# A squeeze-and-excitation block on one core: rows moved 32 at a time instead of 8, cut into small pieces only around the gate

## The chip, the cores and the metric

One core of a Trainium2 chip. The time is the device time of one execution in microseconds; a kernel is judged by the median of its executions. Most executions of one kernel agree closely; a run that is more than 1.5% above the fastest of its kernel is called slow and left out of comparisons.

## The reference

`x` has 256 x 256 pixels of 384 channels in bf16, 50.3 MB. The mean over all pixels goes through two tiny layers and a sigmoid, which gives one factor per channel; every pixel is then multiplied by these factors.

```python
def reference(x, w_down, w_up):
    s = x.mean(axis=(1, 2))
    s = _sigmoid(_silu(s @ w_down) @ w_up)       # 384 -> 24 -> 384
    return x * s[:, None, None, :]
```

No output can be written before all of `x` has been read once. `x` doesn't fit on the core, so a part has to be read a second time.

## The kernel before

A partition holds 512 pixels (called rows here: one row is 384 channels on each of 128 partitions, 98,304 bytes). The kernel works in chunks of 8 rows. 33 chunks (264 rows) have their own slot in SBUF and stay there; the other 31 chunks (248 rows) pass through the same slots first and are read again at the end. The sums over pixels are made by matmuls against a column of ones, one per row.

```python
    JS = 8 if J >= 64 else max(1, J // 8)
    chunks = [(j0, min(JS, J - j0)) for j0 in range(0, J, JS)]
    ...                                       # n_slots comes out as 33, NS as 31
    for (ch, sl) in p1_order:                 # 31 streamed chunks, then 33 that stay
        j0, jsz = chunks[ch]
        st = slots[sl]
        nc.sync.dma_start(out=st[:, :jsz, :], in_=x3[:, j0:j0 + jsz, :])
        for jj in range(jsz):
            ...                               # one matmul per row into sums_ps
    ...
    # the gate: mean (VectorE), transpose (TensorE), copy (VectorE), first layer (TensorE),
    # sigmoid (ScalarE), z1a and z1bc (VectorE), second layer (TensorE), sigmoid (ScalarE)
    def scale_and_store(sl, ch):
        j0, jsz = chunks[ch]
        st = slots[sl]
        gate_b = gate[:, None, :].to_broadcast([P, jsz, C])
        nc.vector.tensor_tensor(
            out=st[:, :jsz, :], in0=st[:, :jsz, :], in1=gate_b, op=ALU.mult
        )
        nc.scalar.dma_start(out=out3[:, j0:j0 + jsz, :], in_=st[:, :jsz, :])

    for i in range(n_slots):
        scale_and_store(i, cache_ids[i])
    for k in range(NS):
        sl = k % n_slots
        j0, jsz = chunks[stream_ids[k]]
        nc.sync.dma_start(out=slots[sl][:, :jsz, :], in_=x3[:, j0:j0 + jsz, :])
        scale_and_store(sl, stream_ids[k])
```

## Time and profile before

The median is 313.33 us (14 executions, 313.16 to 313.70).

| stretch of the profiled execution | us | what limits it |
|---|---|---|
| start to the last load's landing | 125.5 | reading 512 rows, 50.3 MB |
| last landing to the first store's issue | 6.2 | the chain of small steps that makes the gate |
| first store's issue to the end | 180.0 | writing 512 rows and reading 248 again, 74.7 MB |

First come lines of the page of the kernel before. The two long rows are the 40 slices of the span: the busy share of the DMA engines in tenths, and GB/s. Then the shares of the chain that ended last, by engine. Then two groups of instructions (line, engine, operation, output and inputs, count; then busy time in us and mean ns). Last are the DMA issues by line, with count, KB of one and us to landing.

```profile
span 311.8 us, 1476 instructions
...
DMA  7999999999999998099999999999999999999997
GB/s 286 414 417 415 417 419 418 416 418 416 418 415 415 420 418 349 1 365 419 423 419 425 427 422 424 428 423 423 428 426 421 427 426 423 427 426 423 425 427 313
...
DMA 76%; DVE 5%; PE 1%; issue 0%; ACTq 0%; ACT 0%; SPq 0%
...
L175 DVE TENSOR_TENSOR slot<-slot,gate 128x3072 bf16<-128x3072 bf16 x64 | 107.8, 1753 | 20.0 <-DMA slot<-in_x_dram 19.0
L91 PE MATMUL sums_ps<-slot,ones_bf 128*1 128x384 bf16 x512 | 95.4, 331 | 31.7 <-DMA slot<-in_x_dram 31.6
...
slot<-in_x_dram SPq DMA_DIRECT2D x95, 768.0 KB, 15.0
out_dram<-slot ACTq DMA_DIRECT2D x64, 768.0 KB, 14.7
```

The DMA is saturated in every slice but the first, the two in the middle and the last, and most of the chain is transfers. VectorE and TensorE work about 100 us each, hidden behind the transfers. So there are two things to win: a better rate in the 36 good slices, or a shorter hole in the middle.

The stretches view of the kernel before: stretch in us, its length, busy time and (count) of PE, PEld, DVE, ACT and POOL, the granted clock of TensorE (as a share of its full clock), the DMA share (how busy the 16 DMA engines are on average; 1.00 is always) and GB/s. The first stretch is pure reading, the second the first 8 us of stores, the third pure writing.

```profile
20.00:100.00 80.00, 60.65 (x334) 27.70 (x333) 0.00 (x0) 0.00 (x0) 0.00 (x0) 1.00 1.02 417
132.00:140.00 8.00, 0.00 (x0) 0.00 (x0) 8.00 (x6) 0.00 (x0) 0.00 (x0) 0.50 0.94 343
265.00:295.00 30.00, 0.00 (x0) 0.00 (x0) 0.00 (x0) 0.00 (x0) 0.00 (x0) 0.50 1.02 425
```

417 GB/s is the rate of reading, 425 of writing. The hole, as the chain that ended last shows it (start us, us, what):

```profile
110.56 14.99 DMA slot<-in_x_dram
...
125.59 1.47 PE sums_ps L91 x8
...
127.08 0.56 DVE mean_bf L108
...
129.45 0.50 ACT gate L167
...
129.97 11.78 DVE slot L175 x7
```

The last load lands at 125.54 us. Eight matmuls for its rows follow (1.47 us), then the mean and the small steps up to 129.95, then multiplies. Only after the first multiply of 8 rows can the first store go; the timeline of the kernel before has it (start, us, engine, line, operation):

```profile
131.76 21.18 ACTq L178 DMA_DIRECT2D out_dram<-slot  x10
```

131.76 - 125.54 = 6.22 us without any transfer in progress, apart from the latencies at both sides.

### The profile page before, as it was taken

How to read it: one execution, taken by the hardware profiler on the slowest of the kernel's cores; microseconds unless marked ns; L12 is line 12 of the kernel's file. 1: busy time of each engine (PE TensorE's matmuls, PEld its weight loads, DVE VectorE, ACT ScalarE, POOL GpSimd, SP SyncE). 2: the span in 40 equal slices, each digit the busy share in tenths (PEclk: the TensorE clock that was granted, in tenths of full speed). 3: DMA queues.
4: the chain of work that ended last, by engine and by line, in shares of the span. 5: the costliest groups of instructions: out<-in, count | busy, mean ns of one | idle time of the engine just before them, and what ended most of it. 6: DMA issues, size and time to landing. Idle time of an engine off the chain costs nothing.

```text
span 311.8 us, 1476 instructions
## 1 busy us (share of the span) xinstructions
PE 96.1 (31%) x519; PEld 43.7 (14%) x519; DVE 109.0 (35%) x69; ACT 1.9 (1%) x3; POOL 0.2 (0%) x4
## 2 busy tenths in 40 slices
PE   3976777777777777300000000000000000000000
PEld 1432333333333333100000000000000000000000
DVE  0000000000000000499999999999555540000000
ACT  1000000000000000000000000000000000000000
POOL 0000000000000000000000000000000000000000
PEclk9999999999999999855555555555555555555555
DMA  7999999999999998099999999999999999999997
GB/s 286 414 417 415 417 419 418 416 418 416 418 415 415 420 418 349 1 365 419 423 419 425 427 422 424 428 423 423 428 426 421 427 426 423 427 426 423 425 427 313
DMA packets 23371, 125.18 MB, mean 402 GB/s; under 512 B 2988, under 2 KB 3012, under 8 KB 23364
## 3 DMA queue, kind: packets, MB, share of 16 engines
q1 hardware_dynamic: 13680, 74.72, 58.2%
q10 hardware_dynamic: 9684, 50.37, 39.1%
q8 instruction: 4, 0.07, 0.1%
q14 instruction: 3, 0.02, 0.0%
HBM read 74.75 MB, written 50.33 MB: 401 GB/s over the span
## 4 chain that ended last, share of the span: by engine, by line
DMA 76%; DVE 5%; PE 1%; issue 0%; ACTq 0%; ACT 0%; SPq 0%
DMA slot<-in_x_dram 40%; DMA out_dram<-slot 33%; DVE slot L175 4%; DMA wd_sb<-in_w_down_dram 3%; PE sums_ps L91 0%; ACTq L102 0%; DVE mean_bf L108 0%; ACT gate L167 0%; PE zz_ps L160 0%; DVE z1bc L149 0%; PE meanT_ps L118 0%; PE z_ps L136 0%; DVE meanT_sb L127 0%; ACT s L144 0%; DVE z1a L146 0%
## 5 line engine op out<-in xcount | busy, mean ns | idle before, releaser
L175 DVE TENSOR_TENSOR slot<-slot,gate 128x3072 bf16<-128x3072 bf16 x64 | 107.8, 1753 | 20.0 <-DMA slot<-in_x_dram 19.0
L91 PE MATMUL sums_ps<-slot,ones_bf 128*1 128x384 bf16 x512 | 95.4, 331 | 31.7 <-DMA slot<-in_x_dram 31.6
L91 PEld LDWEIGHTS <-ones_bf 128*1 128x1 bf16 x512 | 43.3, 85 | 83.4 <-issue 48.0
L108 DVE TENSOR_SCALAR mean_bf<-sums_ps 1x384 bf16<-1x384 f32 x1 | 0.5, 546 | 126.1 <-PE sums_ps L91 126.1
L144 ACT ACT_TABLE_LOAD x1 | 1.3, 1283 | 3.1 <-issue 3.1
L144 ACT ACTIVATE s<-z_ps 24x1 f32<-24x1 f32 x1 | 0.2, 160 | 124.0 <-PE z_ps L136 124.0
L160 PE MATMUL zz_ps<-wu_sb,z1bc 24*128 24x384 bf16 x1 | 0.3, 332 | 0.7 <-DVE z1bc L149 0.7
L167 ACT ACTIVATE gate<-zz_ps 128x384 bf16<-128x384 f32 x1 | 0.5, 491 | 0.9 <-PE zz_ps L160 0.9
L71 DVE MEMSET ones_bf<- 128x128 bf16 x1 | 0.2, 165 | 0.8 <-PEq L201 0.8
L118 PE MATMUL meanT_ps<-ones_bf,mean_bf 1*128 1x1 bf16 x3 | 0.2, 163 | 0.6 <-DVE mean_bf L108 0.6
L146 DVE TENSOR_TENSOR z1a<-z_ps,s 24x1 f32<-24x1 f32 x1 | 0.1, 145 | 0.5 <-ACT s L144 0.5
L136 PE MATMUL z_ps<-meanT_sb,wd_sb 128*24 128x1 bf16 x3 | 0.2, 163 | 0.3 <-DVE meanT_sb L127 0.3
L118 PEld LDWEIGHTS <-mean_bf 1*128 1x128 bf16 x3 | 0.1, 91 | 1.0 <-DVE mean_bf L108 1.0
L127 DVE CAST meanT_sb<-meanT_ps 128x3 bf16<-128x3 f32 x1 | 0.2, 162 | 0.3 <-PE meanT_ps L118 0.3
L149 DVE TENSOR_SCALAR z1bc<-ones_bf,z1a 24x128 bf16<-24x128 bf16 x1 | 0.2, 242 | 0.0
L136 PEld LDWEIGHTS <-wd_sb 128*24 128x24 bf16 x3 | 0.2, 89 | 0.3 <-issue 0.2
L160 PEld LDWEIGHTS <-z1bc 24*128 24x128 bf16 x1 | 0.1, 91 | 0.8 <-DVE z1bc L149 0.8
L201 POOL MEMSET const-uint8-127<- 128x1 uint8 x1 | 0.1, 102 | 0.0
L201 POOL MEMSET const-bfloat16-1.0<- 128x1 bf16 x1 | 0.1, 101 | 0.0
L201 POOL MEMSET const-float32-0.0<- 128x1 f32 x1 | 0.1, 98 | 0.2 <-issue 0.2
L201 POOL MEMSET const-float32-1.0<- 128x1 f32 x1 | 0.1, 98 | 0.0
## 6 DMA issues: line engine op xcount, KB each, us to landing
slot<-in_x_dram SPq DMA_DIRECT2D x95, 768.0 KB, 15.0
out_dram<-slot ACTq DMA_DIRECT2D x64, 768.0 KB, 14.7
wd_sb<-in_w_down_dram ACTq DMA_DIRECT2D x3, 6.0 KB, 6.2
wu_sb<-in_w_up_dram ACTq DMA_DIRECT2D x1, 18.0 KB
```

Source lines behind the costliest of these rows:

```text
L71: nc.vector.memset(ones_bf[:], 1.0)
L91: nc.tensor.matmul(sums_ps[ci][:1, :csz], ones_bf[:, 0:1], st[:, jj, c0:c0 + csz], start=first, stop=last,)
L108: nc.vector.tensor_scalar(out=mean_bf[:1, c0:c0 + csz], in0=sums_ps[ci][:1, :csz], scalar1=1.0 / float(N), scalar2=None, op0=ALU.mult,)
L118: nc.tensor.matmul(meanT_ps[:csz, kt:kt + 1], mean_bf[0:1, c0:c0 + csz], ones_bf[0:1, 0:1], start=True, stop=True,)
L127: nc.vector.tensor_copy(out=meanT_sb[:, :], in_=meanT_ps[:, :])
L136: nc.tensor.matmul(z1_ps[:R, 0:1], wd_sb[:csz, kt, :], meanT_sb[:csz, kt:kt + 1], start=(kt == 0), stop=(kt == KT - 1),)
L144: nc.scalar.activation(out=s1[:R, :], in_=z1_ps[:R, :], func=ACT.Sigmoid)
L149: nc.vector.tensor_scalar(out=z1bc[:R, :], in0=ones_bf[:R, :], scalar1=z1a[:R, 0:1], scalar2=None, op0=ALU.mult,)
L160: nc.tensor.matmul(zz_ps[:, :csz], z1bc[:R, :], wu_sb[:R, c0:c0 + csz], start=True, stop=True,)
L167: nc.scalar.activation(out=gate[:, c0:c0 + csz], in_=zz_ps[:, :csz], func=ACT.Sigmoid)
L175: nc.vector.tensor_tensor(out=st[:, :jsz, :], in0=st[:, :jsz, :], in1=gate_b, op=ALU.mult)
L201: nc = _bacc.Bacc("TRN2", target_bir_lowering=False, num_devices=1)
```

## The change

The intent: move 32 rows with one DMA, so that each of the 128 runs is 24,576 bytes long and not 6,144, and cut the DMAs and multiplies into small pieces only where somebody waits for the first one (the end of the first pass, the first stores, the first re-reads). The gate's small steps go to ScalarE, one of them is fused, a warm-up activation loads the sigmoid's table at the start, and the two weights move to another queue. The cached and the twice-read rows stay 264 and 248.

```diff
-    JS = 8 if J >= 64 else max(1, J // 8)
+    JS = 32
+    n_slots = 264 // JS
+    spare = 8                     # rows of one more, smaller slot
 ...
+    warm = consts.tile([1, 1], BF16)
+    nc.scalar.activation(out=warm[:], in_=ones_bf[0:1, 0:1], func=ACT.Sigmoid)
 ...
+    for n, (ch, sl) in enumerate(p1_order):
+        remaining = len(p1_order) - n
+        pieces = {1: [4, 2, 2], 2: [8, 8, 8, 4, 4], 3: [16, 16]}.get(remaining)
+        read_and_reduce(ch, sl, pieces)          # one DMA per piece
 ...
-        nc.scalar.dma_start(out=wd_sb[:csz, kt, :], in_=w_down[c0:c0 + csz, :])
+        nc.gpsimd.dma_start(out=wd_sb[:csz, kt, :], in_=w_down[c0:c0 + csz, :])
 ...
-        nc.vector.tensor_scalar(out=mean_bf..., in0=sums_ps..., scalar1=1.0 / float(N), op0=ALU.mult)
+        nc.scalar.activation(out=mean_bf..., in_=sums_ps..., func=ACT.Copy, scale=1.0 / float(N))
 ...
-    nc.vector.tensor_tensor(out=z1a..., in0=z1_ps..., in1=s1..., op=ALU.mult)
-    nc.vector.tensor_scalar(out=z1bc..., in0=ones_bf..., scalar1=z1a..., op0=ALU.mult)
+    nc.scalar.activation(out=z1bc..., in_=z1_ps[:R, 0:1].to_broadcast([R, P]),
+                         func=ACT.Copy, scale=s1[:R, 0:1])
 ...
+    for i in range(n_cache):                      # one multiply and one store per piece
+        scale_and_store(i, cache_ids[i], piece_rows={0: [2, 2, 4, 4, 4, 8, 8],
+                                                     1: [8, 8, 16], 2: [16, 16]}.get(i))
     for k in range(NS):
+        for rsz in {0: [4, 4, 8, 16], 1: [16, 16]}.get(k, [jsz]):   # re-reads
```

More of the change, by code (lines that the diff above doesn't have):

```diff
@@ L36 @@
     cn_chunks = [(c0, min(512, C - c0)) for c0 in range(0, C, 512)]
-    JS = 8 if J >= 64 else max(1, J // 8)
-    chunks = [(j0, min(JS, J - j0)) for j0 in range(0, J, JS)]
-    NCH = len(chunks)
-    bytes_per_slot = JS * C * 2
-    small_bytes = (
-        C * 2
-        + 256
-        + max(32, ((KT * R * 2 + 31) // 32) * 32)
-        + C * 2
-        + C * 2
-        + 8 * 32
-    )
-    avail = nc.sbuf_top - nc.sbuf_base
-    n_slots = max(2, min(NCH, (avail - small_bytes - 2048) // bytes_per_slot))
-    NS = NCH - n_slots
+    JS = 32
+    HALF = JS // 2
+    n_slots = 264 // JS
+    spare = 8
+    cached_rows = n_slots * JS + spare
+    NS = -(-(J - cached_rows) // JS)
+    sizes = [JS] * NS
+    sizes[-1] = J - cached_rows - JS * (NS - 1)
+    sizes += [JS] * n_slots + ([spare] if spare else [])
+    chunks, r = [], 0
+    for sz in sizes:
+        chunks.append((r, sz))
+        r += sz
+    assert r == J
+    NCH = len(chunks)
+    n_cache = NCH - NS
     stream_ids = list(range(NS))
@@ L68 @@
     ]
+    if spare:
+        slots.append(slots_pool.tile([P, spare, C], BF16, name="slot_spare"))
     ones_bf = consts.tile([P, P], BF16)
     nc.vector.memset(ones_bf[:], 1.0)
+    warm = consts.tile([1, 1], BF16)
+    nc.scalar.activation(out=warm[:], in_=ones_bf[0:1, 0:1], func=ACT.Sigmoid)
     sums_ps = [
@@ L78, with read_and_reduce @@
     p1_order = [(stream_ids[k], k % n_slots) for k in range(NS)] + [
-        (cache_ids[i], i) for i in range(n_slots)
+        (cache_ids[i], i) for i in range(n_cache)
     ]
     total_mm = J
-    mm_idx = 0
-    for (ch, sl) in p1_order:
+    mm_state = {"idx": 0}
+    def read_and_reduce(ch, sl, pieces):
         j0, jsz = chunks[ch]
         st = slots[sl]
-        nc.sync.dma_start(out=st[:, :jsz, :], in_=x3[:, j0:j0 + jsz, :])
-        for jj in range(jsz):
-            first = mm_idx == 0
-            last = mm_idx == total_mm - 1
-            for ci, (c0, csz) in enumerate(cn_chunks):
-                nc.tensor.matmul(
-                    sums_ps[ci][:1, :csz],
-                    ones_bf[:, 0:1],
-                    st[:, jj, c0:c0 + csz],
-                    start=first,
-                    stop=last,
-                )
-            mm_idx += 1
+        cuts = []
+        r = 0
+        for pr in pieces or [jsz]:
+            cuts.append((r, pr))
+            r += pr
+        assert r == jsz
+        for (r0, rsz) in cuts:
+            nc.sync.dma_start(
+                out=st[:, r0:r0 + rsz, :], in_=x3[:, j0 + r0:j0 + r0 + rsz, :]
+            )
+            for jj in range(r0, r0 + rsz):
+                first = mm_state["idx"] == 0
+                last = mm_state["idx"] == total_mm - 1
+                for ci, (c0, csz) in enumerate(cn_chunks):
+                    nc.tensor.matmul(
+                        sums_ps[ci][:1, :csz],
+                        ones_bf[:, 0:1],
+                        st[:, jj, c0:c0 + csz],
+                        start=first,
+                        stop=last,
+                    )
+                mm_state["idx"] += 1
@@ L100 @@
+    for n, (ch, sl) in enumerate(p1_order):
+        remaining = len(p1_order) - n
+        pieces = {1: [4, 2, 2], 2: [8, 8, 8, 4, 4], 3: [16, 16]}.get(remaining)
+        read_and_reduce(ch, sl, pieces)
     wd_sb = consts.tile([P, KT, R], BF16)
     for kt, (c0, csz) in enumerate(ck_chunks):
-        nc.scalar.dma_start(out=wd_sb[:csz, kt, :], in_=w_down[c0:c0 + csz, :])
+        nc.gpsimd.dma_start(out=wd_sb[:csz, kt, :], in_=w_down[c0:c0 + csz, :])
     wu_sb = consts.tile([R, C], BF16)
-    nc.scalar.dma_start(out=wu_sb[:R, :], in_=w_up[:, :])
+    nc.gpsimd.dma_start(out=wu_sb[:R, :], in_=w_up[:, :])
@@ L106 @@
     mean_bf = work.tile([1, C], BF16)
     for ci, (c0, csz) in enumerate(cn_chunks):
-        nc.vector.tensor_scalar(
+        nc.scalar.activation(
             out=mean_bf[:1, c0:c0 + csz],
-            in0=sums_ps[ci][:1, :csz],
-            scalar1=1.0 / float(N),
-            scalar2=None,
-            op0=ALU.mult,
+            in_=sums_ps[ci][:1, :csz],
+            func=ACT.Copy,
+            scale=1.0 / float(N),
         )
@@ L126 @@
     if all(csz == P for (c0, csz) in ck_chunks):
-        nc.vector.tensor_copy(out=meanT_sb[:, :], in_=meanT_ps[:, :])
+        nc.scalar.activation(out=meanT_sb[:, :], in_=meanT_ps[:, :], func=ACT.Copy)
     else:
         for kt, (c0, csz) in enumerate(ck_chunks):
-            nc.vector.tensor_copy(
-                out=meanT_sb[:csz, kt:kt + 1], in_=meanT_ps[:csz, kt:kt + 1]
+            nc.scalar.activation(
+                out=meanT_sb[:csz, kt:kt + 1], in_=meanT_ps[:csz, kt:kt + 1],
+                func=ACT.Copy,
             )
@@ L144 @@
     nc.scalar.activation(out=s1[:R, :], in_=z1_ps[:R, :], func=ACT.Sigmoid)
-    z1a = work.tile([R, 1], FP32)
-    nc.vector.tensor_tensor(out=z1a[:R, :], in0=z1_ps[:R, :], in1=s1[:R, :], op=ALU.mult)
     z1bc = work.tile([R, P], BF16)
-    nc.vector.tensor_scalar(
+    nc.scalar.activation(
         out=z1bc[:R, :],
-        in0=ones_bf[:R, :],
-        scalar1=z1a[:R, 0:1],
-        scalar2=None,
-        op0=ALU.mult,
+        in_=z1_ps[:R, 0:1].to_broadcast([R, P]),
+        func=ACT.Copy,
+        scale=s1[:R, 0:1],
     )
@@ L169, with scale_and_store @@
         )
-    def scale_and_store(sl, ch):
+    def scale_and_store(sl, ch, piece_rows=None):
         j0, jsz = chunks[ch]
         st = slots[sl]
-        gate_b = gate[:, None, :].to_broadcast([P, jsz, C])
-        nc.vector.tensor_tensor(
-            out=st[:, :jsz, :], in0=st[:, :jsz, :], in1=gate_b, op=ALU.mult
-        )
-        nc.scalar.dma_start(out=out3[:, j0:j0 + jsz, :], in_=st[:, :jsz, :])
-    for i in range(n_slots):
-        scale_and_store(i, cache_ids[i])
+        if piece_rows is None:
+            cuts = [(0, jsz)]
+        else:
+            cuts = []
+            r = 0
+            for pr in piece_rows:
+                if r >= jsz:
+                    break
+                pr = min(pr, jsz - r)
+                cuts.append((r, pr))
+                r += pr
+            if r < jsz:
+                cuts.append((r, jsz - r))
+        for (r0, rsz) in cuts:
+            gate_b = gate[:, None, :].to_broadcast([P, rsz, C])
+            nc.vector.tensor_tensor(
+                out=st[:, r0:r0 + rsz, :],
+                in0=st[:, r0:r0 + rsz, :],
+                in1=gate_b,
+                op=ALU.mult,
+            )
+            nc.scalar.dma_start(
+                out=out3[:, j0 + r0:j0 + r0 + rsz, :], in_=st[:, r0:r0 + rsz, :]
+            )
+    for i in range(n_cache):
+        scale_and_store(i, cache_ids[i], piece_rows={0: [2, 2, 4, 4, 4, 8, 8], 1: [8, 8, 16], 2: [16, 16]}.get(i))
     for k in range(NS):
@@ L184 @@
         j0, jsz = chunks[stream_ids[k]]
-        nc.sync.dma_start(out=slots[sl][:, :jsz, :], in_=x3[:, j0:j0 + jsz, :])
+        r0 = 0
+        for rsz in {0: [4, 4, 8, 16], 1: [16, 16]}.get(k, [jsz]):
+            nc.sync.dma_start(
+                out=slots[sl][:, r0:r0 + rsz, :], in_=x3[:, j0 + r0:j0 + r0 + rsz, :]
+            )
+            r0 += rsz
+        assert r0 == jsz
         scale_and_store(sl, stream_ids[k])
```

## The prediction

> **What bounds it now.** The page shows DMA at 0.9 or more in all but the first and the middle two of its 40 slices, and the chain that ended last is 76% DMA. 125.05 MB have to move (760 rows read, 512 written, 96 KB each). The stretches view gives 417 GB/s in the load pass, 425 afterwards. The one real hole is the gate: in the chain the last load lands at 125.54 us, then eight matmuls (1.47), small steps up to the gate's end at 129.95, one 8-row multiply (1.75), first store issued at 131.76: 6.2 us. Multiplies (107.8 us) and matmuls (95.4) are hidden.
>
> **What stays.** Bytes are the same: 264 rows cached (8 x 32 + 8), 248 read twice. The sigmoid table load is already at 3.1 us, off the path: the warm-up gains nothing. Weights on another queue gain nothing; they are needed at 128 us.
>
> **Gain 1, the rate.** The trace's packet records: every data packet is 6144 B, one per partition and DMA, 234 ns; a 4-byte packet takes 9 ns, a 48-byte one 11, a 768-byte one 36.5: about 8 ns beside its bytes. In steady state one engine's period is 236 ns (loads), 231 ns (stores). The Trainium skill, "DMA: Bandwidth & Descriptors", gives a ceiling of 435 GB/s (section "Where 436 GB/s comes from"), which is 226 ns for 6144 B, and about 3 cycles of overhead per packet (section "Why small descriptors are slow"); the trace agrees with a residue of 5 to 10 ns, semaphores included. With 32 rows a packet is 24576 B if it stays whole, and the residue is paid a quarter as often. Estimate: loads 417 to 430 GB/s (120.7 to 117 us: -3.7), the rest 425 to 432.5 (74.7 MB: -3.0). If rows are split, or the loads' residue is the HBM's, only part comes. Expected: -5.5.
>
> **Gain 2, the hole.** Two matmuls after the last landing, plus a small backlog (104 rows at 162 ns against 72 landing at 229): about 0.6 instead of 1.47. The fused z1bc and the ScalarE copies save 0.2. The Trainium skill, "ScalarE: Activation LUTs", section "Table sets", says that copy is in every set, so I expect no second table load (1.28 us each). First multiply, 2 rows: 0.55 (1753 ns for 3072 elements, about 0.15 fixed) against 1.75. First store 3.9 us after the last landing instead of 6.2. But 2- and 4-row multiplies deliver 3.6 to 4.2 rows/us, less than DMA takes (4.4), so it starves until re-reads come: about 0.6 given back. Net -1.7.
>
> **Not on the path.** When re-reads start doesn't matter much: stores have over 55 us of backlog, and the kernel ends in a pure store stretch.
>
> **Predicted: 305.5 us**, 8 times in 10 between 301 and 311. Chances: faster by over 2% 0.66, within 2% 0.33, slower 0.01.
>
> **What would show it.** Packets of 24576 B; 428 to 432 GB/s in the load pass, 431 to 434 at the end (if still 417 and 425, gain 1 is wrong); last landing to first store 3.6 to 4.3 us; exactly one table load; the first 10 us of stores somewhat below full rate.
>
> **What would make it wrong.** Rows split into packets of the old length. HBM limiting loads to 417. Matmuls in bursts of 32 with 2 us gaps losing the clock (320 ns each, as at the start), so that a backlog stands at the last landing. Re-reads held back by large stores, so that DMA starves on the DVE for longer. A table load between Copy and Sigmoid.

## The result, and the profile after

The changed kernel has a median of 307.00 us (10 executions, 306.21 to 309.64) against 313.33 (14). The ratio is 0.9813, 95% interval 0.9792 to 0.9835. A ratio here is the mean time of one kernel's fast runs over that of the other's of the same rounds, so it is not quite the ratio of the medians. The interval lies on both sides of 2%, so "faster by over 2%" is neither confirmed nor excluded; that it is faster is clear. Two later sets of five executions gave medians of 307.12 and 306.83.

| stretch of the profiled execution | before | after | difference | predicted |
|---|---|---|---|---|
| start to the last load's landing | 125.5 | 122.3 | -3.2 | -3.7 if packets stay whole |
| last landing to first store | 6.2 | 4.0 | -2.3 | -2.3 |
| first store to the end | 180.0 | 178.1 | -1.9 | -3.0 for the rate, +0.6 for starving |
| span | 311.8 | 304.4 | -7.4 | |

The profiled execution took 306.44 us, one of the fast ones; that of the kernel before took 313.53. The time is longer than the span by 1.8 us before and by 2.1 us after, so of the 7.4 us in the span 7.1 are left in the time. Lines of its page, in the order of those before, with the table load added:

```profile
span 304.4 us, 1259 instructions
...
DMA  8999999999999998299999999999999999999997
GB/s 311 417 430 448 410 436 443 413 429 446 413 432 443 407 417 334 99 371 426 422 426 431 459 388 443 417 452 423 423 452 426 420 449 417 433 443 417 455 420 310
...
L204 DVE TENSOR_TENSOR slot<-slot,gate 128x12288 bf16<-128x12288 bf16 (+5 forms) x25 | 103.1, 4186 | 150.6 <-ACT gate L182 124.7
L105 PE MATMUL sums_ps<-slot,ones_bf 128*1 128x384 bf16 x504 | 90.3, 341 | 31.0 <-DMA slot<-in_x_dram 30.8
...
L75 ACT ACT_TABLE_LOAD x1 | 1.3, 1283 | 0.7 <-PEq L241 0.7
...
slot<-in_x_dram SPq DMA_DIRECT2D x18, 3072.0 KB, 35.2
out_dram<-slot ACTq DMA_DIRECT2D x12, 3072.0 KB, 47.2
```

There are fewer and larger DMAs, and still one table load. The packet records of the trace have runs of 24,576 B, 912 ns each when nothing disturbs them, where there were four of 234 ns (936). The stretches view of the changed kernel, in which 127 to 135 is its first 8 us of stores:

```profile
20.00:100.00 80.00, 60.59 (x343) 29.49 (x341) 0.00 (x0) 0.00 (x0) 0.00 (x0) 0.95 1.01 431
127.00:135.00 8.00, 0.00 (x0) 0.00 (x0) 8.00 (x7) 0.00 (x0) 0.00 (x0) 0.50 0.97 340
265.00:295.00 30.00, 0.00 (x0) 0.00 (x0) 0.00 (x0) 0.00 (x0) 0.00 (x0) 0.50 1.00 433
```

Reading went from 417 to 431 GB/s, writing from 425 to 433. The 431 is a little high, because the edges of a stretch cut long DMAs: undo and coarse below read 428 there. A straight line through the bytes of the packet records gives 417.1 before and 429.5 after for reading (the same in undo and coarse to 0.3), and 425.0 and 432.7 for writing. The granted clock of TensorE in the first stretch is no longer 1.00 but 0.95; an experiment below deals with that. The first 8 us of stores run at 340 GB/s, as before (343). Two stretches of the changed kernel and one of the kernel before show more:

```profile
128.00:129.00 1.00, 0.00 (x0) 0.00 (x0) 1.00 (x2) 0.00 (x0) 0.00 (x0) 0.50 0.81 310
130.00:132.00 2.00, 0.00 (x0) 0.00 (x0) 2.00 (x2) 0.00 (x0) 0.00 (x0) 0.50 1.00 255
...
136.00:140.00 4.00, 0.00 (x0) 0.00 (x0) 4.00 (x4) 0.00 (x0) 0.00 (x0) 0.50 1.03 339
```

At first the DMA engines of the changed kernel are in part idle (share 0.81) while VectorE never rests. From 130 us, when its first re-reads begin (130.75), they are busy all the time and yet move only 255 GB/s; the kernel before has the same dip where its re-reads begin (137.48). Nor is VectorE the slower one: its multiplies of 4 rows start 0.87 us apart (4.6 rows/us), those of 8 rows in the kernel before 1.67 us (4.8), and 432.7 GB/s are 4.4 rows/us. So that the DMA starves on VectorE is not shown, and at most a part of the low rate; why the start of the re-reads costs so much is not shown either. The chain of the changed kernel around the gate:

```profile
105.46 15.93 DMA slot_spare<-in_x_dram
...
121.43 1.47 PE sums_ps L105 x8
...
122.93 0.49 ACT mean_bf L127
...
124.39 0.37 ACT z1bc L165
...
125.17 0.50 ACT gate L182
...
125.70 0.04 DVE slot L204
```

The eight matmuls of the last slot start when its first piece lands (121.39); its last piece lands at 122.33, by the landing records, and the matmuls end 0.57 us later. The 24-partition product is one step of 0.37 us now, and the first multiply is one of 2 rows: it starts at 125.70 and takes 0.56 us, of which only the first 0.04 lie on this chain. The first store is issued at 126.29, 3.96 us after the last landing:

```profile
126.29 19.89 ACTq L210 DMA_DIRECT2D out_dram<-slot  x12
```

### The profile page after: what moved, and what is told of

It reads as the page before. It is cut to its first block, busy times and chain, and to the rows that moved or that the text cites. A ratio compares the mean times of both kernels' runs of the same rounds, so it can differ in the third digit from the quotient of the medians.

```text
span 304.4 us, 1259 instructions
## 1 busy us (share of the span) xinstructions
PE 92.6 (30%) x519; PEld 45.0 (15%) x519; DVE 104.9 (34%) x27; ACT 3.1 (1%) x7; POOL 2.5 (1%) x8
## 4 chain that ended last, share of the span: by engine, by line
DMA 62%; DVE 12%; another core or an unknown queue 5%; PE 3%; issue 1%; SPq 1%; ACT 1%; DVEq 0%
DMA slot<-in_x_dram 47%; DVE slot L204 12%; DMA out_dram<-slot 10%; DMA slot_spare<-in_x_dram 5%; PE sums_ps L105 3%; SPq L98 1%; ACT gate L182 0%; ACT mean_bf L127 0%; ACT z1bc L165 0%; PE zz_ps L175 0%; PE meanT_ps L136 0%; PE z_ps L155 0%; DVEq L204 0%; ACT meanT_sb L145 0%
## 5 line engine op out<-in xcount | busy, mean ns | idle before, releaser
L204 DVE TENSOR_TENSOR slot<-slot,gate 128x12288 bf16<-128x12288 bf16 (+5 forms) x25 | 103.1, 4186 | 150.6 <-ACT gate L182 124.7
L105 PE MATMUL sums_ps<-slot,ones_bf 128*1 128x384 bf16 x504 | 90.3, 341 | 31.0 <-DMA slot<-in_x_dram 30.8
L105 PEld LDWEIGHTS <-ones_bf 128*1 128x1 bf16 x512 | 44.6, 87 | 77.9 <-issue 40.8
L121 POOL DMA_DIRECT2D wd_sb<-in_w_down_dram x3 | 1.8, 602 | 0.8 <-POOLq L241 0.8
L204 DVE TENSOR_TENSOR slot_spare<-slot_spare,gate 128x3072 bf16<-128x3072 bf16 x1 | 1.8, 1753 | 0.0
L105 PE MATMUL sums_ps<-slot_spare,ones_bf 128*1 128x384 bf16 x8 | 1.5, 325 | 0.1
L75 ACT ACT_TABLE_LOAD x1 | 1.3, 1283 | 0.7 <-PEq L241 0.7
```

The costliest lines, as they stand in the source:

```text
L75: nc.scalar.activation(out=warm[:], in_=ones_bf[0:1, 0:1], func=ACT.Sigmoid)
L105: nc.tensor.matmul(sums_ps[ci][:1, :csz], ones_bf[:, 0:1], st[:, jj, c0:c0 + csz], start=first, stop=last,)
L121: nc.gpsimd.dma_start(out=wd_sb[:csz, kt, :], in_=w_down[c0:c0 + csz, :])
L204: nc.vector.tensor_tensor(out=st[:, r0:r0 + rsz, :], in0=st[:, r0:r0 + rsz, :], in1=gate_b, op=ALU.mult,)
```

## The experiments

The kernels of one call share the runs of the kernel before: medians of 313.53, 313.46 and 313.42 us. Two of those runs, of 339.65 and 371.07 us, were slow and are left out. The changed kernel itself was repeated for comparison.

**The theory**: most of the gain comes from longer packets, because each packet costs some nanoseconds beside its bytes; the pieces and the shorter chain around the gate add about 1.5 us. **Rivals**: larger DMAs (more bytes in flight, fewer completions) give the rate, not longer packets; or the gain lies around the gate. A second question came with the result: why do the times of the changed kernel spread over 3 us, when those of the kernel before spread over 0.5?

### again and again2: the changed kernel repeated

No edit.

> The changed kernel unchanged, as the measure for the runs beside it. Median near 307.0 us. If the spread of its times (306.2 to 309.6 before) comes from the tensor engine's clock dropping at a different chunk in each execution, the spread comes again, and a second profile shows the drops at other chunks than the first (34, 69 and 98 us).

> The changed kernel once more, as the measure for the runs beside it: median 307.0 us, times from 306.2 to 309.6. In the profile the 16 landings of the last store should lie 0.5 us apart when the execution is a fast one (306.4) and 2 us or more when it is above 307.8, if single DMA engines that fall behind make the spread.

Measured: again 307.12 us (306.86 to 308.75, ratio 0.9809), again2 306.83 us (306.39 to 308.39, ratio 0.9797). The spread came again. The clock drops of again's profile lie at 33 and 84 us, so at other chunks than in the first profile, but both profiles have the same load pass (last landing 122.28 and 122.33 us) and the same hole (3.92 and 3.96). All of the difference lies after the first store: 179.6 us in again, 178.1 in the first. So the drops seen there cost nothing, and something else made again's profiled execution 1.4 us longer.

The landing records show where. Every DMA is split over 16 engines, and each reports its own landing. For the last store of three profiled executions of this one kernel:

```
execution          last landing   last minus first of the 16 landings
306.44 us          303.19 us      0.5 us
306.97 us          303.7 us       1.6 us
307.87 us          304.63 us      2.4 us
```

In the execution of 307.87 us, 15 engines had finished by 303.42 and one came 1.2 us later. The first landing as late as that is at 147.10 us, 3.5 us after the first of its DMA, the 15th only 0.8 after it. The records don't name the engine, so that it is the same one up to the end is an inference. Nor is a delay there always kept: in the execution of 306.44 us the landings of one store lie 2.1 us apart at 140 us, and 0.5 at the end.

In the load pass engines are late too, and there the traces show with what it comes. The 16 landings of one load lie within 0.6 us of each other at first. After each packet of 16,384 B of the queue that the page calls "instruction" (1.0 to 1.1 us long; in the first profile at 30.2, 61.4, 89.7 and 116.5 us) one more of the 16 is about 1.4 us late: one after the first packet, four after the fourth. All 13 profiles of fast executions have this, with that of the kernel before. In warm and best2 below, whose added matmuls bring six such packets, the first at 11 us, the late landings come earlier as well and are five at the end. So the load pass ends on a few engines, as these stretches of the changed kernel show (DMA share 0.36 and 0.21):

```profile
120.00:121.00 1.00, 1.00 (x9) 0.51 (x7) 0.00 (x0) 0.00 (x0) 0.00 (x0) 1.00 0.36 135
121.00:122.00 1.00, 0.88 (x6) 0.40 (x5) 0.00 (x0) 0.00 (x0) 0.00 (x0) 1.00 0.21 78
```

Both kernels pay this, so it is no part of the gain, and no run tried to avoid it. In the three executions of the table no such packet lies between 117 us and the last landing, so the late engine of the stores has another cause.

### p8: short packets, all else kept

```diff
+    PK = 8
 ...                       # the same at loads, stores and re-reads:
-            nc.sync.dma_start(out=st[:, r0:r0 + rsz, :], in_=x3[:, j0 + r0:j0 + r0 + rsz, :])
+            for q in range(r0, r0 + rsz, PK):
+                qe = min(q + PK, r0 + rsz)
+                nc.sync.dma_start(out=st[:, q:qe, :], in_=x3[:, j0 + q:j0 + qe, :])
```

> Every long load, store and re-read cut into DMAs of 8 rows; slots, matmuls, multiplies and the gate untouched. Packet theory (about 5 to 10 ns per packet beside its bytes): the rates fall back to 417 GB/s in the load pass and 425 afterwards, about 6 us, so 312 to 313.5 us. If the gain of the change lay in the hole around the gate instead, this stays at 307 to 308.

Measured: 312.08 us (311.64 to 312.29), ratio 0.9951. The stretches of pure reading and pure writing:

```profile
20.00:100.00 80.00, 60.81 (x334) 27.77 (x334) 0.00 (x0) 0.00 (x0) 0.00 (x0) 1.00 1.02 417
265.00:295.00 30.00, 0.00 (x0) 0.00 (x0) 0.00 (x0) 0.00 (x0) 0.00 (x0) 0.50 1.02 425
```

The rates are exactly those of the kernel before, while the hole stays at 3.97 us. So the pieces and the new chain alone are worth 313.53 - 312.08 = 1.45 us, and long DMAs the other 5 of the 6.4 us.

### pad8: large DMAs with short packets

The DMAs stay at 3 MB; 32 bytes between blocks of 8 rows in SBUF break every run into four.

```diff
-        slots_pool.tile([P, JS, C], BF16, name=f"slot{i}") for i in range(n_slots)
+        slots_pool.tile([P, JS // 8, 8 * C + 16], BF16, name=f"slot{i}") for i in range(n_slots)
 ...                       # and every access to a slot by blocks, for example
-                out=st[:, r0:r0 + rsz, :], in_=x3[:, j0 + r0:j0 + r0 + rsz, :]
+                out=rows(st, r0, rsz), in_=far(x3, j0 + r0, rsz)
```

> DMAs stay as large as in the changed kernel (3 MB), but 32 bytes between blocks of 8 rows in SBUF break each row of 24576 B into four packets of 6144 B. Theory that packet length sets the rate: as slow as with 8-row DMAs less the few semaphore packets, 417 to 419 and 425 to 427 GB/s, 311 to 313 us. Rival, that the size of a DMA (more bytes in flight, fewer completions) sets it: the rates of the changed kernel, 429 to 433 GB/s, 307 us.

Measured: 311.14 us (310.81 to 311.73), ratio 0.9927; the packet records have 6,144 B again. The stretches:

```profile
20.00:100.00 80.00, 61.41 (x339) 29.66 (x337) 0.00 (x0) 0.00 (x0) 0.00 (x0) 0.94 1.02 419
265.00:295.00 30.00, 0.00 (x0) 0.00 (x0) 0.00 (x0) 0.00 (x0) 0.00 (x0) 0.50 1.02 426
```

Larger DMAs alone raise the rate by 1 to 2 GB/s (419 against 417, 426 against 425) and the time by 0.9 us for the better. Longer packets raise it from 419 to 431 and from 426 to 433 and save 4 us (311.14 against 307.12). The rival falls; packet length is the main cause. By lines through the bytes, reading rises from 418.7 to 429.5 GB/s and writing from 426.0 to 432.7. One packet in place of four saves three, so each costs about 8 ns when read and 5 when written beside its bytes (an estimate from these rates over 16 engines). The 32 bytes also shift the runs in SBUF; p8, whose short runs are not shifted, is no faster, so the shift is not the cause.

### l16: loads with packets of half the length

```diff
-        pieces = {1: [4, 2, 2], 2: [8, 8, 8, 4, 4], 3: [16, 16]}.get(remaining)
+        pieces = {1: [4, 2, 2], 2: [8, 8, 8, 4, 4]}.get(
+            remaining, [16] * (chunks[ch][1] // 16) + [8] * (chunks[ch][1] % 16 // 8))
```

> First pass loaded in DMAs of 16 rows (packets of 12288 B), the rest as in the changed kernel. Packet theory: two thirds of the load gain, 425 to 426 GB/s in the first pass, about 1.1 us longer. Clock theory of the spread: matmuls come in bursts of 16 with 1 us between, the clock never drops after the start, and the times lie within 1 us of each other, around 307.5. If the spread comes from engines of the DMA falling behind each other, it stays near 2 to 3 us.

Measured: 307.52 us (307.14 to 310.01), ratio 0.9835.

```profile
20.00:100.00 80.00, 58.58 (x341) 28.42 (x340) 0.00 (x0) 0.00 (x0) 0.00 (x0) 1.00 1.01 426
```

426 GB/s lies two thirds of the way from 417 to 431 (by lines through the bytes 425.2, between 417.1 and 429.5), as a fixed cost per packet gives: four costs at 6,144 B, two at 12,288 B, one at 24,576 B for the same bytes. The load pass was 1.0 us longer (last landing at 123.30). The clock stayed at 1.00 in this stretch, yet the times spread over 2.9 us, and the two slowest executions (309.34 and 310.01 us) had a mean granted clock of 0.709, above the 0.706 of the profiled one, which had no drop in the load pass. The clock theory of the spread falls.

### warm: filler matmuls

```diff
+    idle_ps = psum.tile([1, P], FP32, name="idle_ps")
 ...
         read_and_reduce(ch, sl, pieces)
+        if pieces is None:
+            for _ in range(16):
+                nc.tensor.matmul(idle_ps[:1, :P], ones_bf[:, 0:1], ones_bf[:, :], start=True, stop=True)
```

> 16 matmuls of 128 columns on constants after each whole chunk of the load pass, into a PSUM tile nobody reads, to fill the 2 us in which the tensor engine waits. Clock theory: no drop to half clock after the first chunk, the times gather near the fastest ones, 306 to 306.6 us, with a spread below 1 us. If the spread comes from elsewhere (DMA), median and spread stay as they are; if the extra matmuls stand in the way, slower.

Measured: 306.61 us (306.33 to 306.79), ratio 0.9779. As an experiment it failed. The fillers depend on no load, so the scheduler put all 224 of them before 26 us, where they fill no gap; the trace still shows a clock drop at 70 us. That the spread was 0.5 us can't be put down to the clock, and why it was so small stays open: best, with the same fillers, spread by 0.45 us in its four fast executions, best2 by 1.0.

### coarse: long rows without the pieces

```diff
-        pieces = {1: [4, 2, 2], 2: [8, 8, 8, 4, 4], 3: [16, 16]}.get(remaining)
+        pieces = None
 ...
-        scale_and_store(i, cache_ids[i], piece_rows={0: [2, 2, 4, 4, 4, 8, 8], 1: [8, 8, 16], 2: [16, 16]}.get(i))
+        scale_and_store(i, cache_ids[i])
 ...
-        for rsz in {0: [4, 4, 8, 16], 1: [16, 16]}.get(k, [jsz]):
+        for rsz in [jsz]:
 ...                       # and the edit of undo, below
```

> Long rows alone: chunks of 32 rows as in the changed kernel, but no pieces at the ends, and the gate's small steps on VectorE as before. Packet theory: the same 429.6 and 432.6 GB/s as the changed kernel, so its traffic is as cheap. But the hole grows: a backlog of the last whole chunk stands at the last landing (32 + 8 matmuls at 162 ns against 8 rows landing in 1.8 us: 4.7 us, not 0.6), and the first multiply is of 32 rows (6.55 us, not 0.55). Hole 14 us instead of 3.9, and 315 to 318 us: slower than the kernel before. If it comes out at 307 to 309, the pieces are for nothing.

Measured: 315.20 us (314.49 to 316.02), ratio 1.0055. The chain that ended last around the gate, and two stretches:

```profile
119.94 8.35 PE sums_ps L103 x40
...
131.28 38.91 DVE slot L207 x6
```

```profile
112.00:119.00 7.00, 5.36 (x32) 2.68 (x32) 0.00 (x0) 0.00 (x0) 0.00 (x0) 1.00 0.98 415
119.00:123.00 4.00, 3.06 (x11) 1.30 (x11) 0.00 (x0) 0.00 (x0) 0.00 (x0) 0.65 0.23 89
```

The rates were those expected (428 and 433 GB/s in the stretches used above). Without pieces the last whole chunk lands at 119.9 and the last 8 rows at 121.73, and 40 matmuls take from 119.94 to 128.29. They took longer than expected because the clock was halved for part of it (0.65 in the second stretch). The first multiply, the first of the six in the last line, is one of 32 rows (6.55 us), and the first store goes at 137.87, 11.6 us later than in the changed kernel: a hole of 16.1 us, where 14 were expected. The profiled execution is the slowest of the four (316.02 us); two others took 1.5 us less, and whether the clock fell in them is not on record. The pieces are what makes the long rows pay.

### undo: the gate's steps, the table warm-up and the weights' queue put back

```diff
-        nc.scalar.activation(out=mean_bf..., func=ACT.Copy, scale=1.0 / float(N))
+        nc.vector.tensor_scalar(out=mean_bf..., scalar1=1.0 / float(N), op0=ALU.mult)
 ...                       # meanT_sb, z1a and z1bc on VectorE, weights on the scalar queue, no warm-up
```

> The changed kernel with the gate's steps back on VectorE, the weights back on the scalar queue and the warm-up activation taken out; chunks and pieces stay. The prediction's point: the small chain is 0.2 us longer, warm-up and weights are worth nothing: 307.0 to 307.5 us, hole 4.1 us. If these parts matter, 308 or more.

Measured: 307.15 us (305.92 to 309.28, four executions), ratio 0.9805. The chain:

```profile
121.35 1.47 PE sums_ps L103 x8
...
124.36 0.15 DVE z1a L164
...
124.55 0.25 DVE z1bc L167
...
125.21 0.50 ACT gate L185
...
125.73 1.97 DVE slot L207 x4
```

From the start of the eight last matmuls to the first multiply it takes 4.38 us (121.35 to 125.73), in the changed kernel 4.27 (121.43 to 125.70). This half of the diff is worth 0.1 us, less than the spread. The profiled execution took 307.99 us, and the landings of its last store lie 2.8 us apart, which fits the explanation of the spread.

### t8: short packets in the 20 us after the gate

```diff
-        piece_rows={0: [2, 2, 4, 4, 4, 8, 8], 1: [8, 8, 16], 2: [16, 16]}.get(i)
+        piece_rows={0: [2, 2, 4, 8, 8, 8], 1: [8, 8, 8, 8], 2: [8, 8, 8, 8]}.get(i)
 ...
-        for rsz in {0: [4, 4, 8, 16], 1: [16, 16]}.get(k, [jsz]):
+        for rsz in {0: [4, 4, 8, 8, 8], 1: [8, 8, 8, 8]}.get(k, [jsz]):
```

> Only the first three stored slots and the first two re-read slots go in DMAs of 8 rows (packets of 6144 B) and multiplies of 8 rows; everything else has long packets. Theory: one engine falls behind the others while long re-read packets and short store packets share it in the 20 us after the gate. Then the spread shrinks below 1 us and the median drops to 306.3 to 306.6. If packet length in that stretch has nothing to do with it, median 307.0 and a spread of 2 to 3 us stay.

Measured: 307.74 us (307.51 to 308.91), ratio 0.9831. It is slower, not faster, and in its profile one engine ends 1.7 us behind the 15th. But this doesn't decide about the mix. From 138 to 164 us, where the packets are now short on both queues, the landings of one DMA lie at most 1.2 us apart; the late one first shows at 176.31, after long packets have set in (from 165.97). The edit moved the mix rather than removing it. What the runs do show is that the spread came with long packets: p8 and pad8, with short ones throughout, spread over 0.7 and 0.9 us (five executions each).

### cache272, best and best2: eight more rows kept

The SBUF has room for 8 more rows, so 240 and not 248 are read twice.

```diff
-    spare = 8                     # rows of one more, smaller slot
+    spare = 16                    # rows of one more, smaller slot
 ...
-        pieces = {1: [4, 2, 2], 2: [8, 8, 8, 4, 4], 3: [16, 16]}.get(remaining)
+        pieces = {1: [8, 4, 2, 2], 2: [8, 8, 8, 4, 4], 3: [16, 16]}.get(remaining)
```

That is cache272; best adds the fillers of warm, best2 these and the pieces of t8 with the first re-reads in pieces of 2, 2, 4 and 8 rows.

> The changed kernel with the filler matmuls of the run warm, and 8 more rows kept in SBUF (272 instead of 264), so that 240 rows and not 248 are read twice. 8 rows are 0.79 MB, 1.8 us at 432 GB/s. Traffic bounds it, so 306.6 less 1.8 = 304.8 us, ratio to before 0.972. If the hole or the stores' start bounded the second part, less than 0.5 us would come.

> 8 more rows kept in SBUF (272), no filler matmuls. Traffic theory: 1.8 us less than the changed kernel, 305.2 us. If the filler matmuls (which all ran before 25 us in the run warm) are what narrowed the spread, this one spreads by 2 to 3 us; if the narrow spread was chance, it says nothing. If the execution of 765 us came from the fillers, none such here.

> 272 rows kept, filler matmuls at the start, and the short packets of t8 after the gate, the first re-reads in pieces of 2, 2 and 4 rows. 304.6 to 305.0 us with a spread below 1 us if t8's theory holds, else as the run best: 305.2.

Measured: best 305.20 us (304.81 to 305.26 in its four fast executions, ratio 0.9732), cache272 305.29 us (305.02 to 306.53, ratio 0.9747, interval 0.9731 to 0.9763), best2 306.25 us (305.97 to 306.95, ratio 0.9779). Against the changed kernel of the same call (306.83), cache272 gains 1.5 us; 8 rows at 432 GB/s are 1.8 us. The traffic does bind, and cache272 beats both kernels. best2, with the pieces of t8 and the finer first re-reads, is 1 us slower than best, about what the pieces cost in t8 (0.9).

One execution of best took 765.2 us, and it is the profiled one. Its stretch from 60 to 580 us:

```profile
60.00:580.00 520.00, 520.00 (x576) 176.97 (x575) 0.00 (x0) 0.00 (x0) 0.00 (x0) 1.00 0.13 52
```

TensorE is busy throughout, its matmuls mostly 1,047 ns apart instead of 162. The 1.00 in the clock column means nothing here: the trace has no clock records for this execution, and the view prints 1.00 then. It is a slow run and used for nothing else. Slow runs of the kernel before were seen as well, though none this slow, and whether the fillers have to do with it stays open. That is one more reason to leave them out.

## Why the prediction was right or wrong

It was right: 307.0 lies in 301 to 311, and the forecast of a faster kernel held; that of over 2% (0.66) stays undecided. The centre, 305.5, was 1.5 us too low. Of this, 0.6 us is in no term: the expected terms, -5.5 and -1.7, give 306.1 from 313.33, and with the full -6.7 for the rate they give 304.9, so that 305.5 is the sum of neither.

1. *The rate is bound by a cost per packet, and longer runs pay it less often.* Right, and shown by taking it away twice (p8, pad8) and halving it once (l16). The prediction named 428 to 432 and 431 to 434 GB/s; the profile has 431 (429.5 by the line through the bytes) and 433. Its cost per packet of 5 to 10 ns fits too: about 5 and 8.
2. *Load pass -3.7 us.* Right in kind, -3.2 in size. Not counted was that the pieces at the end of the pass go at lower rates: the last 40 rows and the 32 before them are in shorter packets, and between 105 and 115 us the stretches view has 417 GB/s. These 72 rows took 16.9 us (105.44 to 122.33), 0.4 more than at 429.5 GB/s.
3. *Hole 6.2 to 3.9 us, 0.6 of it matmuls, no second table load.* Right: 3.96, 0.57 and one load. The Trainium skill, "ScalarE: Activation LUTs", section "Table sets: the hidden batching unit", says that cheap functions are in every set; the trace agrees with one load of 1,283 ns.
4. *Warm-up, weights and ScalarE steps are worth at most 0.2 us.* Right: 0.1 us on the chain (undo).
5. *The pieces of the multiply starve the DMA, 0.6 us given back.* This term was mis-sized. By moved bytes the first 8 us of stores lose 2.5 us against the steady 432.7 GB/s, where the kernel before lost 1.9 against its 425.0: the 0.6 forecast. But its reason, that multiplies of 2 and 4 rows deliver less than the DMA takes, hardly holds: they came at 4.3 (2 rows, twice only) and 4.6 rows/us (4 rows), against the 4.4 it writes. What was not forecast is that the loss grows to 3.6 us in the next 50 us, and only to 2.2 in the kernel before. So 1.4 us were given back in the profiled execution, and 0.9 to 1.3 in those of again2 and again. Why is not shown.
6. *The rest -3.0 us for the rate.* Right as a rate: 74.7 MB take 175.8 us at 425.0 GB/s and 172.7 at 432.7, -3.1. The stretch gained only 1.9 in the profiled execution because of point 5, and 0.4 and 1.3 in those of again and again2. What the prediction missed there is that the kernel ends with the slowest of 16 DMA engines, and that one of them may end up to 2.4 us after the first. That is shown for three executions of this kernel by their landings. But it is not most of the 1.5 us: the execution of 306.44 us has no late engine and is 0.9 over the forecast, so late engines explain at most the 0.6 us by which the median lies above it. Why an engine falls behind in this part is not settled: the clock was tried and fell (l16), and t8 left the packet mix open.
7. *Risk named: bursts of 32 matmuls lose the clock.* They do, in two or three chunks of the first pass, but it cost nothing in the three profiles of the changed kernel, since a later chunk catches up before the end. Where no pieces stand at the end (coarse) it cost 1.7 us (7.04 instead of 5.36 for 32 matmuls).

## What to carry to other kernels

Where a kernel is bound by DMA at a rate a few per cent under the ceiling, look at the packets: lengthen the contiguous run of each partition, not only the DMA. Then make the pieces short just where a chain waits for the first or the last of them; without that, the long DMA costs more than it brings. And count bytes before polishing a chain: two changed lines that kept 8 more rows brought 1.5 us, all of the rewritten gate steps 0.1.

## What the Trainium skill lacked or had wrong

- "DMA: Bandwidth & Descriptors", section "Rules for kernel authors", gives 128 partitions and at least 1 MiB per DMA for the most bandwidth. At 3 MB per DMA the length of the run in a partition still counts: 418.7 GB/s reading and 426.0 writing with 6,144 B runs (pad8), 429.5 and 432.7 with 24,576 B (lines through the bytes). Its section "Why small descriptors are slow" calls putting descriptors together worth it only up to 256 B; here runs four times as long (not short ones put together, but the nearest thing to it) gave 1.6 to 2.6% at 6 KB.
- "TensorE: Matmul & The Clock Gate", section "Why this matters for your kernels", warns of idle gaps over about 3 us. Here the clock halved for 3.4 us after a gap of 1.99 us, with TensorE busy 1.41 of the 3.4 us before; after the gap of 1.94 us before it the clock held. The timeline of the changed kernel (in brackets the idle time before) and the two stretches:

```profile
90.82 5.36 PE L105 MATMUL sums_ps<-slot,ones_bf 128*1 128x384 bf16 x32 [1.94 <-DMA slot<-in_x_dram]
98.17 7.04 PE L105 MATMUL sums_ps<-slot,ones_bf 128*1 128x384 bf16 x32 [1.99 <-DMA slot<-in_x_dram]
```

```profile
95.60:99.00 3.40, 1.41 (x10) 0.60 (x9) 0.00 (x0) 0.00 (x0) 0.00 (x0) 0.99 1.08 463
99.00:102.40 3.40, 3.40 (x12) 1.41 (x11) 0.00 (x0) 0.00 (x0) 0.00 (x0) 0.50 1.01 434
```

- The same page, section "Seeing it yourself", mentions a quarter of the clock for over 50 us. In one execution here matmuls were 6.5 times as far apart as normal (1,047 against 162 ns) for over 400 us. The trace of that execution has no clock records at all, so what the clock was can't be read from it.
- No page that was read says that, with no other data traffic on the core, one of the 16 engines can end late in plain loads and stores from the sync and scalar queues: 2.4 us between the first and the last landing of one store here, against 0.5 us in another execution of the same kernel. Nor does one say that each 16,384 B packet of the instruction queue leaves one more engine about 1.4 us late in a stream of loads (13 profiles).
